# The last four blocks of an attention kernel: o wo 122 and 123 around P V 125 and 126, P 127 in two buffers of its own, last transposes in pairs of 64 rows

## The chip, the cores and the metric

The kernel runs on one core of a Trainium2 chip. Its engines work side by side, each through its own list of instructions in order: TensorE (PE, with PEld for its weight loads) does matrix products and transposes, VectorE (DVE) and ScalarE (ACT) read the products from PSUM, GpSimd (POOL) works on SBUF alone, SyncE (SP) issues most DMAs. The metric is the device time of one execution in microseconds (us). Lower is better.

## The reference, cut to what matters

The input x has 2048 rows of 640 columns. With a layer norm xn of x, 32 heads of 192 columns and a window of the last 512 cached keys and values:

```
q = (xn @ wq) as 32 heads
p = softmax(q kT / sqrt(192))
o = p v
s = o (all heads side by side) @ wo
out = x + s * g
```

g is a silu of xn, changed in two rows that a small routed feed-forward part picks out. That part is finished long before the stretch that the change touches.

## The kernel before, in words

**Blocks.** Attention is cut into 128 blocks (`NB`), numbered 0 to 127. A block is one pair of heads and two row tiles of 128 rows, called its halves `a` = 0 and 1. Four heads make a group (8 groups), and a group's loop runs over four stretches of 512 rows and, in each, over its two pairs of heads, two blocks per pair. All products have 64 rows in contraction, in two row halves `r` = 0 and 1 that run side by side on TensorE and write two PSUM banks.

For a block `b` the steps are:
- `scores` (S, L349): six products into two banks; `row_max` (M, L361): one DVE operation over both.
- `exps` (E, L368): two ACT operations write P in bfloat16 into `p_ring`, which has two places, so block 127 writes where block 125 was. From there a DMA transpose on SP's queue (L376, one per half) writes P's transpose into `pT_ring`. Block 127 takes no DMA: its P goes through TensorE, `p_turn` (U, L381), eight full 128 x 128 transposes per half and one copy per half, on DVE and on ACT.
- `o_products` (P, L389), called P V here: 32 products, 16 per half, from `pT_ring` and v. `o_scaled` (L405) divides by the row sums and writes `o_ring`, on the engines named by two letters. `o_turned` (L417) transposes o by a DMA on SP's queue into `oT_ring`; for blocks 126 and 127 `o_turn` (T, L425) does it on TensorE, six full transposes and one ACT copy.
- o wo: item `k` of 128 is 256 rows (two row tiles) by 320 columns of the output, half its width, for the four heads of a group, 24 products (`w_products`, L437) from the o of two blocks. Items 120 and 121 use blocks 120 and 122, items 122 and 123 blocks 121 and 123, items 124 and 125 blocks 124 and 126, items 126 and 127 blocks 125 and 127. `w_item` (W, L471) sums into `s_acc`. In the last group its products are multiplied by the gate on DVE (`fin_t`), added to what else goes into the output on POOL (`fin_o`, L487), and sent out. `w_last` (L458) does the same for items 124 to 127, with an output DMA of its own for each row tile of an item, the add on DVE (v) or POOL (p) and the output DMA on SP's (s) or ACT's (a) queue, as four letters tell.

**PSUM.** There are three places: "s", two tiles of two banks, which the scores use in turn; "q", one tile of two banks; "o", two tiles of one bank. A step in the last stretch names its place.

**Order.** From block 12 on a loop (`BLOCK`, L962) issues the steps; blocks 126 and 127 and all that is left behind them follow the hand-written list `LAST` (L1017). Every engine keeps the order in which its instructions are issued. In `LAST`, `P.125.vvo` reads: P V of block 125, scaled on DVE and DVE, banks "o". `W.122.s` is o wo item 122 in banks "s"; `W.124.s.vvss` names place, engines and queues; `W.127.0.160.s.vpss` is the first 160 columns of item 127 alone. `U.127.0.qv` turns half 0 of block 127 in banks "q" with a copy on DVE.

**Rings near the end.** `wq_pool` has three tiles for wq; the last one filled serves the queries of blocks 126 and 127. `fin_t` has two tiles of two row tiles each, `fin_o` four tiles of one row tile each, taken in turn: row tiles 14 and 15 of the output (items 126 and 127) take the `fin_o` tiles of row tiles 10 and 11 (items 122 and 123), whose output DMA is issued by POOL (L488).

Of the kernel before, what the change touches and what calls it, by code (L numbers as in the profile page):

```python
# [12 lines left out]
FP32 = mybir.dt.float32  # L13
BF16 = mybir.dt.bfloat16
# [7 lines left out]
def kernel(ctx, tc, A_x, A_k_cache, A_v_cache, A_wq, A_wo, B_x, B_w_r, B_w_gate, B_w_up, B_w_down, out):  # L22
    nc = tc.nc
    P = 128
    _, S, D = A_x.shape
    H = A_k_cache.shape[1]
    Sk = A_k_cache.shape[2]
    Dh = A_k_cache.shape[3]
    W = min(4096, max(256, Sk // 4))
# [4 lines left out]
    DC = D // P  # L34
# [6 lines left out]
    KB = W // HK  # L41
    CC = 2 * Dh // HK
# [14 lines left out]
    def pool(name, bufs, **kw):  # L57
        return ctx.enter_context(tc.tile_pool(name=name, bufs=bufs, **kw))
# [4 lines left out]
    wq_pool = pool("wq", 3)  # L63
# [5 lines left out]
    ps_s = pool("ps_s", 2, space=bass.MemoryType.PSUM)  # L69
# [4 lines left out]
    def f_tile(shape, dtype, name, kind="q"):  # L74
        return banks[kind].tile(shape, dtype, name=name, tag="f")
# [5 lines left out]
    RP, RO, RT, RV, VC = 3, 3, 7, 3, Dh + 8  # L81
    p_ring = big.tile([P, 2, 2, KB, 2, HK], BF16, name="pexp")
    pT_ring = big.tile([P, RP, 2, KB, P], BF16, name="pT")
    o_ring = big.tile([P, RO, CC, 2, HK], BF16, name="o_sb")
    oT_ring = big.tile([P, RT, CC, P], BF16, name="oT")
# [16 lines left out]
    def half(r):  # L102
        return slice(r * HK, (r + 1) * HK)
# [50 lines left out]
    for _ in range(13):  # L154
# [5 lines left out]
        out=ident_f, in_=ident_f, compare_op=ALU.not_equal, fill=1.0, base=0,  # L160
        pattern=[[-1, P]], channel_multiplier=1,
    )
    ident = const.tile([P, P], BF16, name="ident")
# [116 lines left out]
    NB = 2 * NS  # L280
# [68 lines left out]
    def scores(b, a):  # L349
        i = b // 2  # L350
        g, t5, pr = steps[i]
        u = 2 * (b % 2) + a
        s_of[b, a] = ps_s.tile([P, 2, W], FP32, name="s", tag="sc")
        count["S"] += 1
        s_no[b, a] = count["S"]
        for c in range(3):
            for r in range(2):
                nc.tensor.matmul(s_of[b, a][:, r, :], lhsT=qT_of[i][half(r), c, u * P:(u + 1) * P],  # L358
                                 rhs=grp[g][("kT", pr)][half(r), :, c, :], start=(c == 0), stop=(c == 2))
# [5 lines left out]

    split_of = set()

    def exps(b, a, split=False):  # L368
        for hh in range(2):
            nc.scalar.activation(out=p_ring[:, b % 2, a, :, hh, :].rearrange("p (x j) e -> p x j e", x=2),  # L370
                                 in_=s_of[b, a][:, hh, :].rearrange("p (j e x) -> p x j e", j=NJ, x=2),
                                 func=ACT.Exp, bias=nm_of[b, a][:, hh:hh + 1], scale=1.0)
        if a == 0 and split:
            split_of.add(b)
        if b in split_of:
            nc.sync.dma_start_transpose(out=pT_ring[:, b % RP, a], in_=p_ring[:, b % 2, a].rearrange("p k h e -> p (k h e)"))  # L376
        elif a == 1 and b < NB - 1:
            nc.sync.dma_start_transpose(out=pT_ring[:, b % RP].rearrange("p a k t -> p (a k) t"),
                                        in_=p_ring[:, b % 2].rearrange("p a k h e -> p (a k h e)"))

    def p_turn(b, a, where, copy):  # L381
        tp = f_tile([P, KB, P], BF16, "tp_p") if where == "q" else ps_s.tile([P, KB, P], BF16, name="tp_p", tag="sc")
        for k in range(KB):
            nc.tensor.transpose(out=tp[:, k, :], in_=p_ring[:, b % 2, a, k].rearrange("p h e -> p (h e)"), identity=ident)
        copy(out=pT_ring[:, b % RP, a], in_=tp)

    o_of = {}

# [33 lines left out]
        o_scaled(b, engines)  # L422
        o_turned(b)

    def o_turn(b, copy):  # L425
        tp = f_tile([P, CC, P], BF16, "tp_o")
        for c in range(CC):
            nc.tensor.transpose(out=tp[:, c, :], in_=o_ring[:, b % RO, c].rearrange("p a e -> p (a e)"), identity=ident)
        copy(out=oT_ring[:, b % RT], in_=tp)


    def w_of(k):
        sp, up, h = k // 4, (k // 2) % 2, k % 2
        g, t5 = divmod(sp, NT5)
        return g, t5 * 4 + 2 * up, slice(h * HD, (h + 1) * HD), [4 * sp + 2 * pr + up for pr in range(PAIRS)]

    def w_products(k, w_ps, cols=(0, HD)):  # L437
        g, n, cs, bs = w_of(k)
        cs = slice(cs.start + cols[0], cs.start + cols[1])
        for pr in range(PAIRS):  # L440
            for c in range(CC):
                for r in range(2):
                    nc.tensor.matmul(w_ps[r][:, 0:cs.stop - cs.start], lhsT=oT_ring[half(r), bs[pr] % RT, c, :], rhs=grp[g][("wo", pr)][half(r), c, cs],  # L443
                                     start=(pr == 0 and c == 0), stop=(pr == PAIRS - 1 and c == CC - 1))

    def fin_tiles(n):
        if n not in fin_t:
            fin_t[n] = (fin_pool["t"].tile([P, 2, D], FP32, name="fin_t"), [fin_pool["o"].tile([P, D], BF16, name="fin_o") for _ in range(2)])
        return fin_t[n]

    def w_banks(where):
        if where == "o":
            return [f_tile([P, W], FP32, "w", "o") for _ in range(2)]
        w_t = f_tile([P, 2, W], FP32, "w") if where == "q" else ps_s.tile([P, 2, W], FP32, name="w", tag="sc")
        return [w_t[:, u] for u in range(2)]


    def w_last(k, where, how, cols):  # L458
        g, n, cs, _ = w_of(k)
        w_ps = w_banks(where)  # L460
        w_products(k, w_ps, cols)
        cs = slice(cs.start + cols[0], cs.start + cols[1])
        t, o = fin_tiles(n)
        for u in range(2):
            src = w_ps[u][:, 0:cols[1] - cols[0]]
            to = src if how[u] == "v" else t[:, u, cs]
            nc.vector.tensor_tensor(out=to, in0=src, in1=xn[:, n + u, cs], op=ALU.mult)
            (nc.vector if how[u] == "v" else nc.gpsimd).tensor_tensor(out=o[u][:, cs], in0=to, in1=s_acc[:, n + u, cs], op=ALU.add)
            queues[how[2 + u]].dma_start(out=out_v[:, n + u, cs], in_=o[u][:, cs])

    def w_item(k, act=False, where="o"):  # L471
        g, n, cs, _ = w_of(k)
        w_ps = w_banks(where)
        w_products(k, w_ps)
        for u in range(2):
            src, acc = w_ps[u][:, 0:HD], s_acc[:, n + u, cs]
            if g == 0 and act:
                nc.scalar.copy(out=acc, in_=src)
            elif g == 0:
                nc.vector.tensor_copy(out=acc, in_=src)  # L480
            elif g < NG - 1:
                nc.vector.tensor_tensor(out=acc, in0=acc, in1=src, op=ALU.add)  # L482
            else:
                t, o = fin_tiles(n)
                nc.vector.tensor_tensor(out=t[:, u, cs], in0=src, in1=xn[:, n + u, cs], op=ALU.mult)
                if k % 2 == 1:
                    nc.gpsimd.tensor_tensor(out=o[u], in0=t[:, u], in1=s_acc[:, n + u, :], op=ALU.add)  # L487
                    (nc.sync if n >= NTB - 4 else nc.gpsimd).dma_start(out=out_v[:, n + u, :], in_=o[u])  # L488
# [42 lines left out]
    copies = {"a": nc.scalar.copy, "v": nc.vector.tensor_copy}  # L531
# [131 lines left out]
    M = {}  # L663
# [326 lines left out]
    def last(token):  # L990
        op, *n = token.split(".")
        e = [c for c in n if c.isalpha()]
        n = [int(c) for c in n if not c.isalpha()]
        if op == "S":
            scores(*n)
        elif op == "M":
            row_max(*n)
        elif op == "E":
            exps(*n, split=n[0] < NB - 1)
        elif op == "P":  # L1000
            o_products(n[0], where=e[0][2:] or "o")
            o_scaled(n[0], e[0][0:2])
            if n[0] < NB - 2:
                o_turned(n[0])
        elif op == "U":
            p_turn(n[0], n[1], e[0][0], copies[e[0][1]])
        elif op == "T":
            o_turn(n[0], copies[e[0]])
        elif op == "W":
            if len(e) > 1:  # L1010
                w_last(n[0], e[0], e[1], n[1:] or (0, HD))
            else:
                w_item(n[0], where=e[0])
        else:
            flush(n[0])

    LAST = """  # L1017
    B.126 S.126.0 M.126.0 E.126.0 W.120.q S.126.1 M.126.1 E.126.1 P.124.vao S.127.0 M.127.0 W.121.q E.127.0
    B.127 S.127.1 M.127.1 P.125.vvo W.122.s E.127.1 U.127.0.qv U.127.1.sa P.126.avo W.123.s T.126.a P.127.vvo W.124.s.vvss T.127.a W.125.o.ppss W.126.s.ppaa W.127.0.160.s.vpss W.127.160.320.q.vpsa
    """.split()  # L1020
    for token in LAST:
        last(token)
# [31 lines left out]
```

## Time and profile before

| what | value |
|---|---|
| median of 3 runs | 792.28 us (791.06 to 794.29) |
| the profiled execution | 792.27 us |
| its span, first to last instruction | 790.3 us |
| TensorE busy, products | 776.1 us (98% of the span) |
| DVE busy | 580.0 us (73%) |
| ACT busy | 526.5 us (67%) |
| POOL busy | 339.6 us (43%) |
| granted TensorE clock | 1.000 |

The profile is of one execution. Times of events count from the start of the span; the execution's own time is 2.0 us more than the span. Busy times are sums over stages with different limits, and the end of a matrix product is modelled, so that rows of TensorE are best read from start to start. A row of the timeline has start, duration, engine, line, operation, what is written <- what is read, shapes, how many instructions were merged and, in brackets, how long the engine sat idle before and what ended that.

### The profile page before, as it was taken

The numbers are of one execution on the slowest core, as the hardware profiler recorded it, in microseconds if no ns is written. First come the engines' busy times: TensorE is split into PE (matmuls) and PEld (weight loads), VectorE is DVE, ScalarE is ACT, GpSimd is POOL, SyncE is SP. The second block draws the span as 40 slices with busy tenths as digits, with TensorE's granted clock in tenths as the row PEclk, the third lists the DMA queues.
The fourth block names the chain that finished last, engine by engine and source line by source line (L and its number), as shares of the span: only waits on it lengthen the run. The fifth ranks groups of instructions, "written<-read, shape, count | busy, mean of one in ns | idle before, by whom it ended". The sixth has DMA issues, their size and how long they took to land.

```text
span 790.3 us, 27041 instructions
## 1 busy us (share of the span) xinstructions
PE 776.1 (98%) x11380; PEld 572.6 (72%) x11380; DVE 580.0 (73%) x1073; ACT 526.5 (67%) x950; POOL 339.6 (43%) x282
## 2 busy tenths in 40 slices
PE   8899999999999999999999999999999999999997
PEld 4457677777777777777777777777777777777775
DVE  7898788887787767667766766766766776776775
ACT  6676666677666677777666666766666666666661
POOL 1334110023110226626210102569986894266895
PEclk9999999999999999999999999999999999999999
DMA  9989999899999999999999999999999899999993
GB/s 240 196 170 174 174 184 170 146 193 163 175 187 188 211 176 192 191 170 201 175 200 183 194 218 183 158 191 188 165 176 179 149 187 168 182 179 169 181 177 93
DMA packets 447418, 142.18 MB, mean 180 GB/s; under 512 B 414724, under 2 KB 446726, under 8 KB 447296
## 3 DMA queue, kind: packets, MB, share of 16 engines
q1 hardware_dynamic: 437456, 130.84, 99.9%
q10 hardware_dynamic: 8816, 6.76, 3.2%
q0 software_dynamic: 1024, 2.85, 1.4%
q8 instruction: 89, 1.46, 0.8%
q14 instruction: 33, 0.27, 0.1%
HBM read 40.31 MB, written 2.63 MB: 54 GB/s over the span
## 4 chain that ended last, share of the span: by engine, by line
PE 90%; DVE 3%; DMA 3%; ACT 2%; issue 1%; POOL 1%; POOLq 0%; SPq 0%; DVEq 0%; ACTq 0%
PE w L443 25%; PE q_ps L331 24%; PE o_ps L401 20%; PE s L358 19%; DVE nm L363 1%; PE q_ps L300 1%; ACT pexp L370 1%; DMA pT<-pexp 1%; DMA v_sb<-in_A_v_cache_dram 1%; DMA out_dram<-fin_o 1%; DMA oT<-o_sb 0%; ACT xnT L275 0%; POOL fin_o L487 0%; DMA x_in<-in_A_x_dram 0%; PE tp L274 0%
## 5 line engine op out<-in xcount | busy, mean ns | idle before, releaser
L363 DVE TENSOR_REDUCE nm<-s 128x2 f32<-128x1024 f32 x256 | 313.0, 1223 | 137.7 <-PE s L358 135.8
L370 ACT ACTIVATE pexp<-s,nm 128x512 bf16<-128x512 f32 x512 | 324.1, 688 | 97.2 <-DVE nm L363 91.4
L331 PE MATMUL q_ps<-xnT,wq_g 64*128 64x512 bf16 (+1 forms) x2340 | 232.5, 323 | 0.0
L443 PE MATMUL w<-wo_g,oT 64*128 64x320 bf16 (+1 forms) x3096 | 231.4, 295 | 0.1
L358 PE MATMUL s<-kT,qT 64*128 64x512 bf16 x1536 | 211.5, 376 | 2.8 <-ACT pexp L370 2.6
L443 PEld LDWEIGHTS <-oT 64*128 64x128 bf16 x3096 | 170.1, 94 | 58.5 <-DMA oT<-o_sb 0.9
L401 PEld LDWEIGHTS <-pT 64*128 64x128 bf16 x4096 | 177.3, 94 | 31.4 <-issue 2.8
L401 PE MATMUL o_ps<-v_sb,pT 64*128 64x193 bf16 x4096 | 195.4, 243 | 2.9 <-DMA pT<-pexp 2.0
L415 ACT ACTIVATE o_sb<-o_ps,rl 128x192 bf16<-128x192 f32 x246 | 90.1, 418 | 128.8 <-DVE rl L408 128.5
L331 PEld LDWEIGHTS <-wq_g 64*128 64x128 bf16 x2340 | 125.7, 99 | 46.0 <-DVE qT L304 0.5
L149 POOL COPY wo_g<-wo_g 64x1920 bf16<-64x1920 bf16 x32 | 57.3, 1793 | 187.9 <-DMA wo_g<-in_A_wo_dram 165.5
L358 PEld LDWEIGHTS <-qT 64*128 64x128 bf16 x1536 | 84.7, 94 | 58.0 <-issue 3.8
L482 DVE TENSOR_TENSOR s_acc<-s_acc,w 128x320 f32<-128x320 f32 x192 | 85.0, 484 | 31.3 <-PE w L443 31.2
L343 ACT ACTIVATE qT<-q_ps 128x1024 bf16<-128x1024 f32 x114 | 92.4, 811 | 7.1 <-PE q_ps L331 1.0
L412 DVE TENSOR_TENSOR o_sb<-o_ps,rl 128x384 bf16<-128x384 f32 x133 | 74.1, 557 | 4.7
L119 POOL COPY k_perm<-k_raw 128x768 bf16<-128x768 bf16 x30 | 24.3, 826 | 94.1 <-DMA k_raw<-in_A_k_cache_dram 69.7
L893 POOL TENSOR_SCALAR yh<-y_bc,oh 128x640 f32<-128x640 f32 x32 | 60.3, 1884 | 4.7 <-DMA y_bc<-y_d 1.9
L894 POOL TENSOR_TENSOR xn<-xn,yh 128x640 bf16<-128x640 bf16 x32 | 45.0, 1406 | 2.7
L880 POOL TENSOR_TENSOR tz<-tz,xn 128x640 f32<-128x640 f32 x16 | 22.4, 1399 | 54.4 <-ACT tz L879 54.4
L408 DVE RECIPROCAL rl<-o_ps 128x2 f32<-128x2 f32 x256 | 30.7, 160 | 13.6 <-PE o_ps L401 8.9
L953 POOL TENSOR_TENSOR s_acc<-s_acc,x_fin 128x640 f32<-128x640 f32 x16 | 22.4, 1398 | 11.3 <-DMA x_fin<-in_A_x_dram 10.5
L881 POOL TENSOR_TENSOR xn<-tz,xn 128x640 bf16<-128x640 f32 x16 | 22.4, 1398 | 1.3
(140 smaller groups left out, 274.9 us busy)
## 6 DMA issues: line engine op xcount, KB each, us to landing
wo_g<-in_A_wo_dram SPq DMA_DIRECT2D x32, 240.0 KB, 4.1
k_raw<-in_A_k_cache_dram SPq DMA_DIRECT2D x32, 192.0 KB, 3.3
v_sb<-in_A_v_cache_dram SPq DMA_DIRECT2D x32, 192.0 KB, 3.8
wq_g<-in_A_wq_dram SPq DMA_DIRECT2D x14, 288.0 KB, 3.8
pT<-pexp SPq DMA_TRANSPOSE x246, 4.0
wq_g<-in_A_wq_dram SPq DMA_DIRECT2D x14, 192.0 KB, 3.4
x_fin<-in_A_x_dram SPq DMA_DIRECT2D x16, 160.0 KB, 3.8
oT<-o_sb SPq DMA_TRANSPOSE x126, 3.6
```

The source lines that it names most:

```text
L149: nc.gpsimd.tensor_copy(out=grp[g][("wo", pr)][half(1), cs, :], in_=grp[g][("wo", pr)][half(0), cs, :])
L331: mm = nc.tensor.matmul(q_ps[k][:, 0:n] if type(q_ps) is list else q_ps[:, k, 0:n], lhsT=wq[half(r), dc, c:2 * Dh:3], rhs=xnT[half(r), tok ...
L343: nc.scalar.activation(out=out, in_=q_ps[:, :, 0:n], func=ACT.Copy, scale=scale)
L358: nc.tensor.matmul(s_of[b, a][:, r, :], lhsT=qT_of[i][half(r), c, u * P:(u + 1) * P], rhs=grp[g][("kT", pr)][half(r), :, c, :], start=(c = ...
L363: rm = nc.vector.tensor_reduce(out=nm_of[b, a], in_=s_of[b, a], axis=AX.X, op=ALU.max, negate=True)
L370: nc.scalar.activation(out=p_ring[:, b % 2, a, :, hh, :].rearrange("p (x j) e -> p x j e", x=2), in_=s_of[b, a][:, hh, :].rearrange("p (j ...
L401: nc.tensor.matmul(o_of[b][r][:, a, 0:Dh + 1], lhsT=pT_ring[half(r), b % RP, a, k, :], rhs=v_ring[half(r), (g * PAIRS + pr) % RV, k, 0:Dh ...
L412: nc.vector.tensor_tensor(out=o_sb, in0=src, in1=rl[:, r].unsqueeze(2).unsqueeze(3).to_broadcast([P, 2, 3, HK]), op=ALU.mult)
L415: nc.scalar.activation(out=o_sb[:, a], in_=src[:, a], func=ACT.Copy, scale=rl[:, r, a:a + 1])
L443: nc.tensor.matmul(w_ps[r][:, 0:cs.stop - cs.start], lhsT=oT_ring[half(r), bs[pr] % RT, c, :], rhs=grp[g][("wo", pr)][half(r), c, cs], sta ...
L482: nc.vector.tensor_tensor(out=acc, in0=acc, in1=src, op=ALU.add)
L893: nc.gpsimd.tensor_scalar(out=yh, in0=M["y_bc"][:, j, :], scalar1=M["oh"][:, n, j:j + 1], scalar2=None, op0=ALU.mult)
```

## The change

- **Order (`LAST`).** o wo 122 moves ahead of P V 125 and of the last two exps. o wo 123 stays behind P V 126. The steps now use other banks: o wo 122 "o" (was "s"), P V 125 "q" (was "o"), o wo 123 "q" (was "s"), the turned P "s", the turned o "s" (was "q"), and the last four items "q", "s", "o", "q".
- **P of block 127** goes into two tiles taken from `wq_pool`, one per half, where it went into `p_ring`'s place of block 125.
- **Transposes on TensorE.** `p_turn` turns both halves of block 127 at once, 16 pairs of transposes of 64 rows to 64 columns, the members of a pair into two banks; each bank is copied by one operation, one on ACT and one on DVE. `o_turn` does the same with six pairs and two copies, both on ACT.
- **Scaling.** P V 125 and 127 are scaled on ACT and DVE (were on DVE alone).
- **The last items.** Item 127 is one piece of 320 columns (was two of 160). Adds: item 124 POOL and DVE (was DVE twice), 125 POOL twice, as before, 126 POOL and DVE (was POOL twice), 127 POOL and DVE (was DVE and POOL in either piece). One output goes through ACT's queue (were three), seven through SP's.

```
+    def p_of(b, a):
+        if b < NB - 1:
+            return p_ring[:, b % 2, a]
+        if a not in p_last:
+            t = wq_pool.tile([P, DC, 2 * Dh], BF16, name="wq_g")
+            p_last[a] = t.rearrange("p c d -> p (c d)")[:, 0:KB * P].rearrange("p (k h e) -> p k h e", k=KB, h=2)
+        return p_last[a]
...
-    def p_turn(b, a, where, copy):
-        tp = f_tile([P, KB, P], BF16, "tp_p") if where == "q" else ps_s.tile([P, KB, P], BF16, name="tp_p", tag="sc")
-        for k in range(KB):
-            nc.tensor.transpose(out=tp[:, k, :], in_=p_ring[:, b % 2, a, k].rearrange("p h e -> p (h e)"), identity=ident)
-        copy(out=pT_ring[:, b % RP, a], in_=tp)
+    def two_banks(where, dtype, name):
+        n = W * 4 // mybir.dt.size(dtype)
+        if where == "o":
+            return [f_tile([P, n], dtype, name, "o") for _ in range(2)]
+        t = f_tile([P, 2, n], dtype, name) if where == "q" else ps_s.tile([P, 2, n], dtype, name=name, tag="sc")
+        return [t[:, r] for r in range(2)]
+
+    def p_turn(b, es, where):
+        tp = [t.rearrange("p (a k t) -> p a k t", a=2, k=KB) for t in two_banks(where, BF16, "tp_p")]
+        for a in range(2):
+            for k in range(KB):
+                for r in range(2):
+                    nc.tensor.transpose(out=tp[r][:, a, k, :], in_=p_of(b, a)[half(r), k].rearrange("p h e -> p (h e)"), identity=ident[half(r), half(r)])
+        for r in range(2):
+            copies[es[r]](out=pT_ring[:, b % RP, :, :, half(r)], in_=tp[r])
...
-    def o_turn(b, copy):
-        tp = f_tile([P, CC, P], BF16, "tp_o")
+    def o_turn(b, es, where):
+        tp = [t[:, 0:CC * P // 2].rearrange("p (c t) -> p c t", c=CC) for t in two_banks(where, BF16, "tp_o")]
         for c in range(CC):
-            nc.tensor.transpose(out=tp[:, c, :], in_=o_ring[:, b % RO, c].rearrange("p a e -> p (a e)"), identity=ident)
-        copy(out=oT_ring[:, b % RT], in_=tp)
+            for r in range(2):
+                nc.tensor.transpose(out=tp[r][:, c, :], in_=o_ring[half(r), b % RO, c].rearrange("p a e -> p (a e)"), identity=ident[half(r), half(r)])
+        for r in range(2):
+            copies[es[r]](out=oT_ring[:, b % RT, :, half(r)], in_=tp[r])
...
     LAST = """
     B.126 S.126.0 M.126.0 E.126.0 W.120.q S.126.1 M.126.1 E.126.1 P.124.vao S.127.0 M.127.0 W.121.q E.127.0
-    B.127 S.127.1 M.127.1 P.125.vvo W.122.s E.127.1 U.127.0.qv U.127.1.sa P.126.avo W.123.s T.126.a P.127.vvo W.124.s.vvss T.127.a W.125.o.ppss W.126.s.ppaa W.127.0.160.s.vpss W.127.160.320.q.vpsa
+    B.127 S.127.1 M.127.1 W.122.o E.127.1 P.125.avq U.127.avs P.126.avo W.123.q T.126.aas P.127.avo W.124.q.pvss T.127.aas W.125.s.ppss W.126.o.pvss W.127.q.pvsa
     """.split()
```

`exps` and `p_turn` now find P through `p_of`; `w_last` and `w_item` take their banks from `two_banks`, which does for them what `w_banks` did.

More of the change, by code (lines that the diff above doesn't have):

```diff
@@ L366 @@
     split_of = set()
+    p_last = {}
+    def p_of(b, a):
[5 more added lines that the diff above has]
+        return p_last[a]
     def exps(b, a, split=False):
         for hh in range(2):
-            nc.scalar.activation(out=p_ring[:, b % 2, a, :, hh, :].rearrange("p (x j) e -> p x j e", x=2),
+            nc.scalar.activation(out=p_of(b, a)[:, :, hh, :].rearrange("p (x j) e -> p x j e", x=2),
                                  in_=s_of[b, a][:, hh, :].rearrange("p (j e x) -> p x j e", j=NJ, x=2),
@@ L375, in exps @@
         if b in split_of:
-            nc.sync.dma_start_transpose(out=pT_ring[:, b % RP, a], in_=p_ring[:, b % 2, a].rearrange("p k h e -> p (k h e)"))
+            nc.sync.dma_start_transpose(out=pT_ring[:, b % RP, a], in_=p_of(b, a).rearrange("p k h e -> p (k h e)"))
         elif a == 1 and b < NB - 1:
@@ L449, in fin_tiles @@
         return fin_t[n]
[L451 to L455, printed above, removed]
     def w_last(k, where, how, cols):
         g, n, cs, _ = w_of(k)
-        w_ps = w_banks(where)
+        w_ps = two_banks(where, FP32, "w")
         w_products(k, w_ps, cols)
@@ L472, in w_item @@
         g, n, cs, _ = w_of(k)
-        w_ps = w_banks(where)
+        w_ps = two_banks(where, FP32, "w")
         w_products(k, w_ps)
@@ L1005, in last @@
         elif op == "U":
-            p_turn(n[0], n[1], e[0][0], copies[e[0][1]])
+            p_turn(n[0], e[0][0:2], e[0][2])
         elif op == "T":
-            o_turn(n[0], copies[e[0]])
+            o_turn(n[0], e[0][0:2], e[0][2])
         elif op == "W":
```

## The prediction, on record before the result

> **What bounds the kernel now.** I read the page first, then the waits of the last 29 us, then TensorE's timeline there.
>
> ```profile
> span 790.3 us, 27041 instructions
> PE 90%; DVE 3%; DMA 3%; ACT 2%; issue 1%; POOL 1%; POOLq 0%; SPq 0%; DVEq 0%; ACTq 0%
> ```
>
> TensorE carries 90% of the chain that ended last. Up to the row maxima of block 127 every engine's order stays as it was, so all that the change can win or lose lies behind 764 us of the span. Who waits there:
>
> ```profile
> ACT pexp L370 <- DMA pT<-pexp: 2.1, 1, 2.1
> PE o_ps L401 <- DMA pT<-pexp: 1.8, 1, 1.8
> ```
>
> The second line is TensorE's only idle stretch there. TensorE's own timeline (start, duration, work) shows where:
>
> ```profile
> 764.78 1.81 PE L443 MATMUL w<-wo_g,oT 64*128 64x320 bf16 x24
> 766.41 0.83 PE L358 MATMUL s<-kT,qT 64*128 64x512 bf16 x6
> 767.06 0.85 PE L401 MATMUL o_ps<-v_sb,pT 64*128 64x193 bf16 x16
> 769.67 0.84 PE L401 MATMUL o_ps<-v_sb,pT 64*128 64x193 bf16 x16 [1.77 <-DMA pT<-pexp]
> 770.35 1.79 PE L443 MATMUL w<-wo_g,oT 64*128 64x320 bf16 x24
> 772.08 1.07 PE L384 MATMUL tp_p<-ident,pexp 128*128 128x128 bf16 x16
> 773.08 1.51 PE L401 MATMUL o_ps<-v_sb,pT 64*128 64x193 bf16 x32
> 774.42 1.79 PE L443 MATMUL w<-wo_g,oT 64*128 64x320 bf16 x24
> 776.15 0.51 PE L428 MATMUL tp_o<-ident,o_sb 128*128 128x128 bf16 x6
> 776.59 1.51 PE L401 MATMUL o_ps<-v_sb,pT 64*128 64x193 bf16 x32
> 777.93 1.79 PE L443 MATMUL w<-wo_g,oT 64*128 64x320 bf16 x24
> 779.66 0.51 PE L428 MATMUL tp_o<-ident,o_sb 128*128 128x128 bf16 x6
> 780.10 5.09 PE L443 MATMUL w<-wo_g,oT 64*128 64x320 bf16 x96
> ```
>
> Read start to start, the rows are: o wo of 121, scores of 127, the two halves of P V of 125, o wo of 122, the sixteen transposes of P 127, P V 126, o wo 123, transposes of o 126, P V 127, o wo 124, transposes of o 127, then o wo 125 to 127. The one hole is between the halves of P V 125. The second half waits for a DMA transpose:
>
> ```profile
> 763.08 6.54 DMA pT<-pexp
> 767.62 1.84 SPq L376 DMA_TRANSPOSE pT<-pexp  x1
> pT<-pexp SPq DMA_TRANSPOSE x1, 3.9
> DMA to landing us min/median/max: 3.3/4.2/6.5
> ```
>
> The chain has P of 125's second half landing at 763.08 + 6.54 = 769.62. The next two rows are the queue's last transpose of P (126, second half) and its time to landing: 767.62 + 3.9 = 771.5. The last line spans all transposes of P behind 750 us.
>
> **Unit costs from these rows.** o wo followed by scores, both of 64 rows, takes 766.41 - 764.78 = 1.63 us. o wo followed by full transposes takes 772.08 - 770.35 = 1.73: entering the 128-row form costs 0.10. Sixteen transposes take 1.00 and six 0.44, so one is 0.56 / 10 = 0.056, and 1.00 - 16 x 0.056 = 0.10 is left for the way back. A whole P V takes 774.42 - 773.08 = 1.34, a half 0.68.
>
> In the Trainium skill, TensorEngine Tiling (Array Packing), Key Properties, changing the tiling mode drains TensorE. The trace agrees, at 0.10 us a change.
>
> **Part 1: o wo 122 ahead of P V 125.** Its inputs are older than block 125, and its banks are now those of P V 124, whose last reader is this ACT row:
>
> ```profile
> 765.57 0.73 ACT L415 ACTIVATE o_sb<-o_ps,rl 128x192 bf16<-128x192 f32 x2
> 767.44 1.21 DVE L363 TENSOR_REDUCE nm<-s 128x2 f32<-128x1024 f32 x1
> 769.71 1.27 ACT L370 ACTIVATE pexp<-s,nm 128x512 bf16<-128x512 f32 x2 [2.10 <-DMA pT<-pexp]
> 773.18 1.01 ACT L385 COPY pT<-tp_p 128x1024 bf16<-128x1024 bf16 x1 [2.20 <-PE tp_p L384]
> ```
>
> Free at 766.30, needed at 767.06: no wait. So o wo 122 runs 767.06 to 768.69, P V 125's first half to 769.36, a stall of 0.31 is left, and the second half runs 769.67 to 770.35. The transposes of P 127 then start at 770.35 instead of 772.08: **1.73 gained** (1.63 of the stall, 0.10 of a change of form).
>
> **Part 2: P 127 in its own buffers.** The last two exps no longer wait for 769.62. Row maxima end at 768.65, so exps end near 768.68 + 1.27 = 769.95, ahead of 770.35. Without this part, exps would end at 770.98 while the second eight transposes want P at 770.35 + 0.45 = 770.8: it is worth about 0.2 in the new order, and nothing in the old one. The buffers are former wq tiles whose last products lie blocks back: no wait.
>
> **Part 3: transposes as pairs of 64 rows.** Three groups lose two changes of form each; 0.10 of these six is in part 1, so 0.50 remains. Instructions double: 16 full transposes become 16 pairs, 6 become 6, twice, 28 pairs in all. No row shows a 64-row transpose. From below, 64 columns at o wo's rate (12 pairs of 320 columns in 1.63, so 0.136 a pair) are 0.027 a pair. From above, a pair with 193 columns takes 1.34 / 16 = 0.084; if the halves don't overlap, two full transposes are 0.112. I take **0.056**, the full transpose's own time, since the same 128 columns of weights are loaded per member, and loads of a pair demonstrably fit beside each other in 0.084. Each 0.01 more costs 0.28 in all.
>
> Copies: one of 1.0 on ACT and one on DVE for P 127 as before; two of 384 columns on ACT for each o, done in about 1.1 (estimate: 768 columns at the 1.01 per 1,024 of the row above, and 0.3 for a second start). From the end of either group of transposes to the half of o wo that reads them lie at least 2.1 (774.56 to 775.90 + 0.82), so they hide. Were that cover gone, the second copy's 0.3 would show.
>
> TensorE after: P 127 turned 770.35 to 771.25; P V 126 to 772.59 (its second half at 771.92 needs the 771.5 landing: 0.4 spare); o wo 123 to 774.22; o 126 turned to 774.56; P V 127 to 775.90; o wo 124 to 777.53; o 127 turned to 777.87. Before, that point was 780.10, so **2.23 are gained**. o wo 125, 126 and 127, whole, at 1.63: the last starts at 781.13.
>
> **Part 4: the tail.** o wo 127 goes in one piece, and the finishing work moves between DVE and POOL.
>
> ```profile
> 776.26 0.89 DVE L485 TENSOR_TENSOR fin_t<-w,xn 128x320 f32<-128x320 f32 x2 [0.81 <-PE w L443]
> 776.84 1.54 POOL L487 TENSOR_TENSOR fin_o<-fin_t,s_acc 128x640 bf16<-128x640 f32 x1 [3.06 <-DVE fin_t L485]
> 778.67 0.56 POOL L488 DMA_DIRECT2D out_dram<-fin_o  x1 [0.30 <-POOL fin_o L487]
> 779.25 1.54 POOL L487 TENSOR_TENSOR fin_o<-fin_t,s_acc 128x640 bf16<-128x640 f32 x1
> 779.84 0.50 DVE L467 TENSOR_TENSOR w<-w,xn 128x320 f32<-128x320 f32 x1 [0.21 <-PE w L443]
> 780.43 0.49 DVE L468 TENSOR_TENSOR fin_o<-w,s_acc 128x320 bf16<-128x320 f32 x1
> 781.09 0.56 POOL L488 DMA_DIRECT2D out_dram<-fin_o  x1 [0.30 <-POOL fin_o L487]
> 782.52 2.56 POOL L468 TENSOR_TENSOR fin_o<-fin_t,s_acc 128x320 bf16<-128x320 f32 x3 [0.88 <-DVE fin_t L467]
> 787.09 0.34 ACTq L469 DMA_DIRECT2D out_dram<-fin_o  x1
> ```
>
> DVE starts 1.9 behind the start of an o wo (779.84 - 777.93). For o wo 127 that is 783.03: multiply for POOL, 0.41 later (0.89 less the 0.49 of one) the multiply for itself, 0.59 later its add of 0.49, so 784.52. POOL: its chain for row tiles 10 and 11 now starts at 772.59 + 1.9 + 0.58 = 775.07 and frees it 2 x 2.41 later, 779.9; five adds of 0.85 follow, four by 783.3, the last from 783.58 to 784.44. Neither waits long for the other. The last output is issued at about 784.55, against 787.09: **2.54 gained**, 2.23 of it TensorE's, 0.3 the balance of the tail.
>
> ```profile
> out_dram<-fin_o POOLq DMA_DIRECT2D x5, 160.0 KB, 2.4
> out_dram<-fin_o SPq DMA_DIRECT2D x4, 80.0 KB, 1.7
> out_dram<-fin_o SPq DMA_DIRECT2D x3, 40.0 KB, 1.7
> 781.09 4.03 DMA out_dram<-fin_o
> ```
>
> The last pieces are twice as big, but 80 KB land as fast as 40 KB, so the 3.2 us between last issue and span's end stay. Span 790.3 - 2.54 = 787.76; the execution itself 792.27 - 2.54 = **789.7 us**. The median before is 792.28, so 0.01 separates profile and median.
>
> **Rivals.**
> 1. *A new wait on a slow landing.* The output tile that DVE adds into for o wo 126 is that of row tile 11, whose DMA POOL issues at about 779.31. DVE wants it at 782.4. With the median 2.4 it lands at 781.7, with the 4.03 of this trace at 783.34. DVE waits in order, so o wo 127's three operations queue behind: last issue near 785.37, gain 1.72, **790.6**. Before, POOL did this add late enough not to mind. For it: the last row. Against it: the median.
> 2. *Pairs as dear as two full transposes*, 0.112: 28 x 0.056 = 1.57 lost, **791.3**. The Trainium skill, TensorEngine Tiling (Array Packing), Instruction Overhead, speaks for it: every matmul bears about 60 cycles, and one should not split a dimension that is already small. The pairs of P V, with two loads in 0.084, speak against it.
> 3. *Slower than before:* members of a pair run one after the other, each behind its own load. The page's loads take
>
> ```profile
> L401 PEld LDWEIGHTS <-pT 64*128 64x128 bf16 x4096 | 177.3, 94 | 31.4 <-issue 2.8
> ```
>
> 94 ns, so a pair takes 0.188, 28 x 0.132 = 3.70 is lost, **793.4**. It decides from 0.056 + 2.54 / 28 = 0.147 a pair. Against it: the same loads overlap in every P V.
> 4. *The change covers a stall that usually is not there.* If that transpose lands in the median 4.2 (767.3), the stall in the median run is nil, and 2.54 - 1.63 = 0.9 is all: **791.4**. Against it: profile and median agree to 0.01.
> 5. *More than forecast:* pairs at 0.027 gain 0.81 more on TensorE, until the landing at 771.5 stops P V 126: **789.0**.
>
> **How the numbers follow.** Forecast 0.60 (own range 789.2 to 790.3); rivals 0.13, 0.12, 0.04, 0.05, 0.06 in this order. From 789.0 to 791.4 lie all but rival 3; the three runs of before spread by -1.2 and +2.0 about their median, and about 0.8 of that is added below and above: 788.2 to 792.2. Half a per cent is 3.96 us, about what a measurement of this kernel can tell from no change; the forecast gain of 2.5 stays inside. Faster by more needs under 788.3, rival 5 or the forecast with run spread in its favour: 0.10. Slower by more needs over 796.2, beyond even rival 3: 0.03. Within: 0.87.
>
> **What would show it.** Right: no wait of P V above 0.4 us behind 764 us; the P V 126 row about 1.7 to 1.9 earlier; no idle weight load ahead of transposes; 28 pairs near 0.056. Wrong: DVE's fin_o add of o wo 126 idle before it on DMA out_dram (rival 1); pair groups of 1.8 or 3 us for P 127 instead of 0.9 (rivals 2, 3); the same hole elsewhere, above all ahead of P V 126's second half; or last output issued less than 2 us earlier although TensorE ends 2.2 earlier, which would mean that POOL's five adds bound the tail.

## The result and the profile after

| | kernel before | changed kernel |
|---|---|---|
| first comparison, median of 5 runs | 791.25 us (791.01 to 794.29) | 788.05 us (787.67 to 788.91) |
| its ratio | | 0.9953, 95% interval 0.9934 to 0.9972 |
| second comparison, median | 792.03 us (29 runs) | 789.56 us (12 runs) |
| its ratio | | 0.9971, interval 0.9962 to 0.9981 |
| span of the first profile | 790.3 us | 787.1 us |

The ratios are of means. So the change brings 3.2 us by the medians of the first comparison and 2.5 by those of the second (3.7 and 2.3 by the ratios), within half a per cent in both. The forecast was a gain of 2.5 and a time of 789.7, in a range of 788.2 to 792.2: the first median lies 0.15 us below that range. The page of the changed kernel:

```profile
span 787.1 us, 27038 instructions
PE 92%; DVE 3%; DMA 2%; ACT 2%; issue 0%; SPq 0%; DVEq 0%; ACTq 0%
```

TensorE's share of the chain grew from 90% to 92% and DMA's fell. TensorE's timeline of the changed kernel, from the second scores of block 127 on:

```profile
766.86 0.83 PE L358 MATMUL s<-kT,qT 64*128 64x512 bf16 x6
767.51 1.81 PE L467 MATMUL w<-wo_g,oT 64*128 64x320 bf16 x24
769.14 1.51 PE L423 MATMUL o_ps<-v_sb,pT 64*128 64x193 bf16 x32
770.47 0.65 PE L405 MATMUL tp_p<-ident,wq_g 64*128 64x64 bf16 x32
770.94 1.51 PE L423 MATMUL o_ps<-v_sb,pT 64*128 64x193 bf16 x32
772.57 1.81 PE L467 MATMUL w<-wo_g,oT 64*128 64x320 bf16 x24
774.20 0.35 PE L451 MATMUL tp_o<-ident,o_sb 64*128 64x64 bf16 x12
774.37 1.51 PE L423 MATMUL o_ps<-v_sb,pT 64*128 64x193 bf16 x32
777.33 0.35 PE L451 MATMUL tp_o<-ident,o_sb 64*128 64x64 bf16 x12
777.51 5.07 PE L467 MATMUL w<-wo_g,oT 64*128 64x320 bf16 x72
```

Three things are to be seen. P V 125 is one group of 32 with no hole. Sixteen pairs of transposes take 770.94 - 770.47 = 0.47 us, 0.029 a pair; six take 0.17 to 0.18. And from P V 126 to o wo 123 it is 772.57 - 770.94 = 1.63, where a P V takes 1.34: a new hole of 0.29. VectorE's timeline and the weight loads show where it comes from:

```profile
770.69 0.17 DVE L430 RECIPROCAL rl<-o_ps 128x2 f32<-128x2 f32 x1 [0.40 <-PE o_ps L423]
771.66 0.17 DVE L430 RECIPROCAL rl<-o_ps 128x2 f32<-128x2 f32 x1 [0.80 <-ACT o_sb L437]
771.87 0.56 DVE L434 TENSOR_TENSOR o_sb<-o_ps,rl 128x384 bf16<-128x384 f32 x1
772.56 0.69 DVE L407 COPY pT<-tp_p 128x1024 bf16<-128x1024 bf16 x1
773.17 0.23 DVE L430 RECIPROCAL rl<-o_ps 128x2 f32<-128x2 f32 x2
```
```profile
772.54 1.50 PEld L467 LDWEIGHTS <-oT 64*128 64x128 bf16 x24 [0.32 <-PE o_ps L423]
```

P V 125 now lies in banks "q", one PSUM tile of two banks. Ahead of its second reciprocal DVE stands idle for 0.80 until ACT has read the other bank, and the banks come free at 772.43. P V 126 is scaled on the same two engines out of two tiles, and its two reciprocals (773.17) follow each other without a wait. o wo 123 takes the banks of P V 125 and starts at 772.57. (The last row names PE as releaser, since P V 126 ended at about the same time, 770.94 + 1.51 = 772.45; the runs that change the banks or the scaling, below, tell the two apart.)

The end, on DVE, POOL and ACT's queue:

```profile
783.68 0.49 DVE L486 TENSOR_TENSOR fin_o<-w,s_acc 128x320 bf16<-128x320 f32 x1
```
```profile
779.83 4.22 POOL L486 TENSOR_TENSOR fin_o<-fin_t,s_acc 128x320 bf16<-128x320 f32 x5
```
```profile
784.24 0.37 ACTq L487 DMA_DIRECT2D out_dram<-fin_o  x1
```

POOL ends at 784.05, DVE at 784.17: balanced, as worked out. From the last issue to the span's end it is 2.9 us, where the kernel before took 3.2.

### The profile page after: what moved, and what is told of

It reads as the page before. It is cut to its first block, busy times and chain, and to the rows that moved or that the text cites. A ratio compares the mean times of both kernels' runs of the same rounds, so it can differ in the third digit from the quotient of the medians.

```text
span 787.1 us, 27038 instructions
## 1 busy us (share of the span) xinstructions
PE 774.5 (98%) x11384; PEld 573.3 (73%) x11384; DVE 578.8 (74%) x1068; ACT 527.9 (67%) x956; POOL 339.3 (43%) x281
## 4 chain that ended last, share of the span: by engine, by line
PE 92%; DVE 3%; DMA 2%; ACT 2%; issue 0%; SPq 0%; DVEq 0%; ACTq 0%
PE w L467 26%; PE q_ps L331 24%; PE o_ps L423 21%; PE s L358 20%; DVE nm L363 1%; PE q_ps L300 1%; ACT pexp L380 1%; DMA oT<-o_sb 1%; DMA x_in<-in_A_x_dram 1%; DMA v_sb<-in_A_v_cache_dram 1%; PE tp L274 0%; ACT o_sb L437 0%; ACT xnT L275 0%; PE gu_ps L821 0%; DVE stats L523 0%
## 5 line engine op out<-in xcount | busy, mean ns | idle before, releaser
L467 PE MATMUL w<-wo_g,oT 64*128 64x320 bf16 x3072 | 231.4, 296 | 0.2
```

## The experiments

The order of the program up to block 127's second scores is the same in every kernel here, yet they start anywhere from 766.33 to 769.66 in the 14 profiles. That spread of 3.3 us hides most of what is sought, so every profile is read from the start of those scores ("stretch"), and times serve as a check. A ratio is to the kernel before as timed beside that run.

| run | scores to o wo 125 | scores to last output issue | ratio to before |
|---|---|---|---|
| before, four profiles | 13.69, 13.17, 12.59, 12.26 | 20.68, 20.22, 19.37, 19.17 | 1 |
| changed, two profiles | 10.65, 10.65 | 17.38, 17.38 | 0.9953; 0.9971 |
| order only | 11.75 | 18.52 | 0.9978 (0.9968 to 0.9988) |
| pairs only | 10.91 | 17.92 | 0.9982 (0.9971 to 0.9993) |
| changed, no pairs | 11.75 | 18.70 | 0.9979 (0.9964 to 0.9993) |
| changed, o wo 123 in "s" | 10.61 | 17.33 | 0.9965 (0.9951 to 0.9979) |
| changed, P 127 in its old place | 10.65 | 17.38 | 0.9963 (0.9949 to 0.9978) |
| changed, old last items | 10.65 | 17.68 | 0.9985 (0.9975 to 0.9994) |
| changed, P V 125 on DVE alone | 10.35 | 17.09 | 0.9983 (0.9972 to 0.9994) |
| changed, o 126 moves 128 columns | 10.81 | 17.54 | profile only |

**Order alone.** Full transposes, P 127 in its old place, old scaling engines, old last items:

```
+    ... M.127.1 W.122.o E.127.1 P.125.vvq U.127.vas P.126.avo W.123.q T.126.aas P.127.vvo
+    W.124.q.vvss T.127.aas W.125.s.ppss W.126.o.ppaa W.127.0.160.s.vpss W.127.160.320.q.vpsa
```

> The kernel before with o wo 122 and 123 around P V 125 and 126 and the banks that this needs; full 128 x 128 transposes, P 127 in its old place, old scaling engines and old last items. Measured from the start of block 127's second scores to the last output issue, the kernel before took 20.68 us and the changed one 17.38. Theory A (order, pairs and tail are terms that add up on TensorE's path): this run takes 20.68 - 1.7 to 2.1 = 18.6 to 19.0, time about 2 us under the kernel before; P V 125 shows a hole of at most 0.4. Theory B (the hole is the whole gain, the pairs only move a wait): it takes about 17.5, time 3 us under.

```profile
767.15 0.83 PE L358 MATMUL s<-kT,qT 64*128 64x512 bf16 x6
...
769.42 1.51 PE L422 MATMUL o_ps<-v_sb,pT 64*128 64x193 bf16 x32
770.87 1.07 PE L404 MATMUL tp_p<-ident,pexp 128*128 128x128 bf16 x16
```

No hole in P V 125, and 18.52: just under theory A's 18.6 to 19.0, 1 us over what theory B gave. B falls. The 1.45 ahead of the full transposes, against 1.33 ahead of the pairs, is the change of form again.

**Pairs alone**, in the old order:

```
+    ... M.127.1 P.125.vvo W.122.s E.127.1 U.127.avs P.126.avo W.123.s T.126.aaq P.127.vvo
+    W.124.s.vvss T.127.aaq W.125.o.ppss W.126.s.ppaa W.127.0.160.s.vpss W.127.160.320.q.vpsa
```

> The kernel before with the pairs of 64 rows alone, in the old order, P 127 in its old place, old last items. Theory A: 28 pairs at 0.029 instead of 0.056 and six changes of form at 0.10 go: 0.76 + 0.6 = 1.3 us less, stretch 19.3 to 19.5, and the hole ahead of P V 125's second half is still there (1 to 1.8). Theory B: stretch 20.3 or more, time within 0.5 us of the kernel before.

```profile
769.07 0.84 PE L423 MATMUL o_ps<-v_sb,pT 64*128 64x193 bf16 x16 [0.36 <-DMA pT<-pexp]
...
771.38 0.63 PE L405 MATMUL tp_p<-ident,pexp 64*128 64x64 bf16 x32
771.85 1.50 PE L423 MATMUL o_ps<-v_sb,pT 64*128 64x193 bf16 x32
```

The stretch of 17.92 misses A's 19.3 to 19.5, because the hole was 0.36 and not 1.77, with nothing edited ahead of it. Put the first profile's hole back (1.4) and it is 19.3. So the hole differs by execution, which three more profiles of the unedited kernel were to show.

**The kernel before, three more profiles**, no edit.

> The kernel before, unedited, for one more profile: how long is the hole ahead of P V 125's second half from execution to execution? Theory (its size is set by when that DMA transpose lands, which eight profiles of kernels with the same order up to there put 1.8 to 3.2 us behind the start of block 127's second scores): the second half starts 0.05 behind the landing, loses 0.5 to 1.9, most often about 0.9, and the stretch from the scores to the last output issue is 18.74 plus this loss. Rival: the 1.9 of the first profile is the rule, and the landings of the other kernels are early because they were edited: stretch 20.5 to 20.8.

> As the run before: the unedited kernel before, a second further profile. Theory: the loss lies between 0.5 and 1.9 and differs from the other profiles; rival: 1.7 to 2.0 again.

> As the run before: the unedited kernel before, a third further profile. Theory: the loss lies between 0.5 and 1.9 and differs from the other profiles; rival: 1.7 to 2.0 again.

One line of the waits of each:

```profile
PE o_ps L401 <- DMA pT<-pexp: 1.3, 1, 1.3
```
```profile
PE o_ps L401 <- DMA pT<-pexp: 0.7, 1, 0.7
```
```profile
PE o_ps L401 <- DMA pT<-pexp: 0.3, 1, 0.3
```

With the first profile the waits are 1.8, 1.3, 0.7 and 0.3. Each costs about 0.17 more start to start, so 1.94, 1.42, 0.84 and 0.51 are lost, 1.2 on average. The first profile was the worst of four, and the rival, that 1.9 is the rule, falls. Up to o wo 125 each of the four takes 11.75 plus what it loses, and the order alone takes 11.75: the new order wins the hole and no more. The pairs alone take 10.91 with 0.53 lost, so 10.38 without the hole: they win 1.37.

**Full transposes in the changed kernel:**

```
-    for r in range(2):
-        nc.tensor.transpose(out=tp[r][:, a, k, :], in_=p_of(b, a)[half(r), k]..., identity=ident[half(r), half(r)])
+    nc.tensor.transpose(out=tp[a][:, k, :], in_=p_of(b, a)[:, k]..., identity=ident)
```

(and the same for o, with one copy).

> The changed kernel with full 128 x 128 transposes and one copy per o. Theory A: 1.3 us come back less the 0.29 by which o wo 123 waits in the changed kernel, which the longer transposes cover: stretch 17.38 + 1.0 = 18.4, time about 1 us over the changed kernel. Theory B: within 0.3 us of the changed kernel.

To o wo 125 it takes 11.75 - 10.65 = 1.10 longer, as theory A has it. The last issue comes 1.32 later, and the other 0.22 is seen on DVE:

```profile
785.39 0.49 DVE L483 TENSOR_TENSOR fin_o<-w,s_acc 128x320 bf16<-128x320 f32 x1 [0.50 <-DMA out_dram<-fin_o]
```

That is rival 1 of the prediction, in a run where the landing took 3.8 us.

**o wo 123 in the scores' banks:** `W.123.q` becomes `W.123.s`.

> The changed kernel with o wo 123 in the scores' banks instead of those of P V 125. Theory A on the new hole (o wo 123 waits until P V 125 is scaled out of the same banks): the 0.29 us between P V 126 and o wo 123 go, stretch 17.1, time 0.3 us under the changed kernel, which the times alone can't show. Rival (TensorE waits there for something else, as its weights or a drain): the hole of 0.29 stays.

```profile
773.19 1.81 PE L467 MATMUL w<-wo_g,oT 64*128 64x320 bf16 x24
775.07 0.35 PE L451 MATMUL tp_o<-ident,o_sb 64*128 64x64 bf16 x12
```

The hole ahead of o wo 123 is gone, but o wo 123 to the transposes of o 126 now takes 1.88 and not 1.63. DVE still stands 0.80 for ACT, so o 126 is scaled late. Only 0.05 is won: the banks were where the wait showed, not what made it.

**P V 125 scaled on DVE alone:** `P.125.avq` becomes `P.125.vvq`.

> The changed kernel with P V 125 scaled on DVE alone. In the changed kernel DVE's second reciprocal for block 125 stands idle for 0.80 until ACT has scaled its half, both halves being one PSUM tile there; P V 125's banks are read out 1.9 us behind its end, and o wo 123, which takes them, starts 0.29 late. With DVE alone nothing waits for ACT: read out 1.45 + 0.2 behind its end, at 5.3, o wo 123 starts at 5.41 with no hole, and o 126 is scaled by 6.9 ahead of its transposes at 7.04. Stretch 17.38 - 0.29 = 17.1, time 0.3 us under the changed kernel. Rival: DVE now has 0.7 more work, so its copy of P 127 and the scaling of o 126 come later, and the hole moves to the transposes of o 126, as it did with o wo 123 in the scores' banks: stretch 17.3 to 17.5.

```profile
766.33 0.83 PE L358 MATMUL s<-kT,qT 64*128 64x512 bf16 x6
...
771.74 1.81 PE L467 MATMUL w<-wo_g,oT 64*128 64x320 bf16 x24
773.37 0.35 PE L451 MATMUL tp_o<-ident,o_sb 64*128 64x64 bf16 x12
```

773.37 - 771.74 = 1.63, and P V 126 to o wo 123 took 1.34: neither hole is left, and the stretch is 17.09, 0.29 shorter as expected. The times don't show it: the median is 790.62 (11 runs) against 789.56 (12 runs) for the unedited changed kernel beside it, with intervals that overlap. It has the shortest stretch of all; that it is faster isn't shown.

**P 127 in its old place:** `p_of` returns `p_ring[:, b % 2, a]` for every block.

> The changed kernel with P of block 127 in its old place. The last two exps wait for the landing of P 125's second half, which the earlier profiles put 1.8 to 3.2 us behind the start of block 127's second scores; exps want to start at 2.27. If it lands by 2.27 (four of five profiles), nothing changes: stretch 17.3 to 17.5. If it lands at 3.2, exps end at 4.5, the second half of the transposes starts at 4.5 instead of 3.85, and the stretch is 0.3 to 0.7 longer. Theory A: the buffers are an insurance worth 0 to 0.7. Rival: they are worth the 2.1 us that ACT waited in the kernel before.

17.38, to the hundredth that of the changed kernel. The transpose landed 2.16 behind the scores, ahead of the exps. The buffers paid nothing here; a landing at 3.2, as in the first profile of before, is what they insure against, and no run showed that case.

**Old last items** (banks as the new order needs):

```
+    W.124.q.vvss T.127.aas W.125.s.ppss W.126.o.ppaa W.127.0.160.s.vpss W.127.160.320.q.vpsa
```

> The changed kernel with the last four o wo items as before (DVE, POOL, queues, item 127 in two pieces). Theory A: TensorE up to o wo 125 as in the changed kernel (10.65 from the scores), the stretch behind it 6.99 as before instead of 6.73: about 17.65, 0.27 more. Rival (the new tail is where the unforeseen 0.7 us came from): 0.7 or more.

0.29 longer to the last issue, as theory A says. But from the last issue to the end of the span it takes 3.27, against 2.89 and 2.79 in the two profiles of the changed kernel. So the tail is worth 0.3 + 0.4 to 0.5 against this run; the second part was in neither sum.

The first part differs by profile. From o wo 125 to the last issue it takes 6.78 to 7.04 in the seven profiles with the old items, 6.94 on average, and 6.72 to 6.74 in six of the seven with the new ones (6.96 in the run without pairs, with its late landing). That is 0.04 to 0.31, 0.2 on average.

The second part doesn't differ, and the traces' semaphore records show most of what makes it. A semaphore is the counter that tells an engine of a landing. At the end SP waits for the outputs' eight semaphores one after the other, in the same order in every trace, about 0.06 us each. The old items send ten outputs through SP and ACT, so the last two to be issued count on the first two semaphores of that list, and from the wait for the last issued output to the end of the span it is 1.28 us in all seven profiles. The new items send eight, the last one stands last in the list, and it is 0.90 or 0.91 in all seven.

**The changed kernel once more.**

> The changed kernel once more, unedited, beside its variants. Theory A: stretch 17.4 with a hole of 0.29 ahead of o wo 123 and none ahead of P V 125; time 2.5 to 3.5 us under the kernel before. Rival: the 3.2 us of its first timing were partly chance, and it comes out less than 2 us under.

2.5 us by the medians, the lower end of what theory A gave, and 2.3 by the ratio, a little under it and over the rival's 2; and the same stretch to 0.01. By the ratio the first comparison has the gain at 2.2 to 5.2 us and this one at 1.5 to 3.0, so they agree between 2.2 and 3.0.

**Columns moved or weights loaded.** The transposes of o as plain products with the unit matrix. Weights are the same 64 x 128; for o 126 each member moves 128 columns, of which 64 are zeros that a neighbour overwrites, for o 127 it moves 64:

```
+    cols = half(r) if b == NB - 1 else slice(0, P)
+    nc.tensor.matmul(tp[r][:, c0:c0 + cols.stop - cols.start], lhsT=o_ring[half(r), b % RO, c]..., rhs=ident[half(r), cols], start=True, stop=True)
```

> The changed kernel with the pairs for o 126 and o 127 as plain products with the unit matrix into 32-bit PSUM: for o 126 each member moves 128 columns (the 64 that count, and 64 of zeros, which a neighbour overwrites), for o 127 it moves 64. Weights loaded are the same 64 x 128 in both. Theory (a pair's time is that of the columns moved): 0.056 a pair for o 126, 0.029 for o 127. Rival (the step of the prediction: the load of the weights sets it): the same time for both.

```profile
775.43 0.52 PE L454 MATMUL tp_o<-ident,o_sb 64*128 64x128 bf16 x12
775.76 1.51 PE L423 MATMUL o_ps<-v_sb,pT 64*128 64x193 bf16 x32
...
778.73 0.35 PE L454 MATMUL tp_o<-ident,o_sb 64*128 64x64 bf16 x12
778.90 2.35 PE L470 MATMUL w<-wo_g,oT 64*128 64x320 bf16 x32
```

Six pairs take 0.33 with 128 columns and 0.17 with 64: 0.055 and 0.029 a pair. The columns moved set it: 64 more cost 0.026, so all but some 0.003 of the 0.029 goes with the columns.

## Why the prediction was right and wrong, step by step

The direction held, and the size nearly: 2.54 forecast, 3.2 and 2.5 measured by the medians. By the stretches it is 19.86 (the mean of four) - 17.38 = 2.48 to the last issue, and 0.3 to 0.4 behind it. The sum came out by errors that cancel, and the time fell out of the range.

- **Part 1, "1.73 gained ... a stall of 0.31 is left".** The mechanism was right: o wo 122 fills the hole, in every profile of the new order. The size was one execution's: on average 1.2 is lost to the hole, and 0.1 to the change of form, so 1.3 is gained and no stall is left. Rival 4 (the stall usually isn't there), given 0.05, was half right.
- **Part 2, "worth about 0.2 in the new order".** Nothing in the run that undid it.
- **Part 3, "I take 0.056, the full transpose's own time, since the same 128 columns of weights are loaded per member".** This step failed. Loads don't set the time of a pair, the 64 columns moved do: 0.029, near the lower end that the prediction worked out. 28 x 0.027 = 0.76 more is gained, which is rival 5, given 0.06. The changes of form were sized right: six at 0.10 and 0.76 make 1.36, and undoing the pairs cost 1.10 and covered the hole of 0.29, together 1.39. Rivals 2 and 3 fall with it. The Trainium skill, TensorEngine Tiling (Array Packing), Instruction Overhead, gives each matmul some 60 cycles of overhead; as a cost on top of the columns moved, no run here shows it. The two copies of o took 0.86 together, where 1.1 was estimated, and hid: a second start costs 0.06 more than the one copy of 0.80 before, not 0.3.
- **A wait that the prediction did not see:** scaling on two engines out of one PSUM tile, 0.80 on DVE and 0.29 on TensorE. The prediction checked that each bank was read out in time by adding up durations, and took ACT and DVE to run beside each other, as they do for P V 126 in two tiles.
- **Part 4:** the balance of the tail, 0.3 forecast, was 0.29 in the run with the old items and 0.2 on average. "The 3.2 us between last issue and span's end stay" failed: 2.8 to 2.9. It goes with the new last items, since all seven profiles with the old ones took 3.20 to 3.27; most of it is SP's row of waits behind the last output (1.28 against 0.90 or 0.91), a term that the prediction doesn't have.
- **Rival 1** did not happen in the changed kernel: its landing took 2.08. It did, at 0.5 us, in the run without pairs. "Before, POOL did this add late enough not to mind" was close: in the kernel before the landing came at 785.12, POOL's add began at 785.25 with 0.17 idle ahead of it, and the chain that ended last runs through that landing.
- **The range** was laid about 792.27, the profiled execution. The kernel before had a median of 791.25 in the first comparison, and 28 pairs at the wrong price were 0.76 more; either of the two put right would have held the time inside. Put right, the terms up to the last issue are 1.28 for part 1, 0.50 and 0.76 for part 3, 0.29 lost to the new wait and 0.20 for the balance, 2.45 in all, where 2.48 was measured: that the forecast's 2.54 lies so near is luck.

## What to carry to other kernels

A hole that ends with a DMA's landing is a draw from a distribution: take several profiles before its size goes into a sum, and measure edits of the last microseconds from a mark that comes just before them. Short products in row pairs cost what they move, here down to 64 columns, and saving the change of form comes on top. When a step moves to other banks, ask whether its two readers share one PSUM tile there: the wait turns up on an engine that isn't the bound, and then where TensorE needs that engine's result. At the end of a program count the outputs, and ask in which order their landings are waited for.

## What the runs showed of the hardware

**The last 160 KB output through POOL's queue landed in 3.7 to 4.1 us or in 2.1 to 2.2.** It is the second output of row tiles 10 and 11. It took 3.7 to 4.1 us in the four profiles of the kernel before and in the run without pairs, and 2.07 to 2.20 in the nine others. The DMA view of the kernel before from 781.7 to 784.7 (issue 781.09, landing 785.12), and that of the changed kernel from 779.3 to 781.4 (issue 779.24, landing 781.32):

```profile
q0 software_dynamic: 48, 0.16, 15.7%
q8 instruction: 1, 0.02, 3.2%
```
```profile
q0 software_dynamic: 48, 0.16, 21.1%
```

In all five late cases one 16 KB instruction packet began 1.3 to 1.8 us behind the issue, while the output's packets were moving, and in eight of the nine others none fell there; in the ninth one began 1.87 behind, as the last of the output's packets ended. That the packet holds up one DMA engine's share is one reading; it wasn't tried by itself. The run without pairs fits it badly: there the packet began 1.82 behind, when most of the punctual outputs had moved their last packet (1.72 to 1.76).

**The same order of work starts its last stage 766.33 to 769.66 us into the span.** What spreads it isn't known; it is about as much as the whole change brings.
